# Order of the heads in the stored queries and keys, and loading of the staged tiles, in a transformer block

## The chip, the cores and the metric

The kernel runs on one core of one Trainium2 chip. The metric is the device time of one execution in microseconds. Five engines take part. TensorE (PE in the profile) multiplies matrices, VectorE (DVE) reduces and does elementwise work, ScalarE (ACT) copies and applies functions, GpSimd (POOL) takes some elementwise work, and SyncE (SP) issues most of the transfers between the main memory and the on-chip memory. Each engine works through its own instructions in order and waits on semaphores for the others.

## The reference

The program is one pre-norm transformer block in float32 on 2048 tokens of width 640, with 32 heads of 20 dimensions:

```
h   = x + softmax(q k^T / sqrt(20)) v @ wo        q, k, v = heads of layernorm(x) @ wqkv
out = h + (silu(z @ w_gate) * (z @ w_up)) @ w_down   with z = layernorm(h)
```

The softmax is over all 2048 keys, and every head needs the maximum of each row of scores.

## The kernel before

Precision is kept by splitting: a float32 matrix is written as a high and a low part, and a product is made of three partial products. A staged head holds three rows per dimension for the same reason, 60 rows in all, and two heads stand side by side on the partitions (rows 0 to 63 and 64 to 127), each with two positions along the free axis. So one tile holds one group of four heads.

The program has three stages: the projections (to about 362 us in the profile), the attention, and the feed-forward part. All that the change touches is in the projections and in the loads of queries and keys, `stack` (L111).

**Stage of projections.** The tokens are cut into four chunks `c` of 512. For each chunk the loop at L466 walks through 18 *slots*; slot number `18*c + j` is kept in `slot[0]` (L472). A slot is a "block" (`query_key`, L373: 15 matmuls of 512 columns that make 128 rows of queries or of keys) or a "value" (L414: 15 matmuls of 320 columns). Chunk 0 does blocks in slots 0 to 9 and values in slots 10 to 17; chunks 1 and 2 do likewise (18 to 27 and 28 to 35; 36 to 45 and 46 to 53); chunk 3 does its keys first (54 to 58), then values (59 to 66), then queries (67 to 71). After a block, `keep` (L395) copies the result to a tile `e`, splits it and hands it to `store` (L367), which issues it from ScalarE's queue at the next `keep`, to the DRAM tensor `qk_d`. There a group has 80 rows per part, sorted by dimension and, within it, by head.

**Row maxima beside the projections.** Part of the score maxima is computed during this stage, between the projections' matmuls. `max_pair` (L141) is one unit of it, called a pair below: two matmuls (L146) into one of three `ps_wide` buffers and a reduction on VectorE (L150). There are 208 pairs. `visit(n)` (L301) issues up to n of them from two queues: `urgent` (unit 0, from the tiles `k_stk` and `q_stk`) and `early`. A block has two visits of two pairs, after its tenth matmul and at its end; a value has one of three.

**Staged tiles.** For most `early` pairs, of head groups 1 to 7 and chunks 0 and 1, queries and keys are read back from `qk_d` into tiles `raw`. Their pool has four buffers, which also hold the raw weights early on (`load_w`, L311). A *set* (L238) is a group, a chunk of queries and a chunk of keys: 21 sets. `load_staged` (L254) takes two buffers per set and issues eight transfers, four by each of two calls of `stack`, all from SP's queue. The load of set i+1 is issued when the first pair of set i is issued (`first_keys`, L271), and not before the slot given by `ready_at` (L241). It uses the two buffers of set i-1, so SP waits for the last pair of that set. A set has 8 pairs, but only 4 or 6 where chunk 1 is set against the second chunk of keys. A pair whose slot has come is issued whether or not its tile has landed, and TensorE waits for it then. Queries of chunk 1 are loaded twice, once per set.

**The transfer.** In `stack`, a transfer of `n` partitions reads two heads per partition, `b` and `b + 2`: of the 4n stored rows of n dimensions it takes every second one, 2n rows at one even step, into n partitions of two pieces of 2 KB.

Of the kernel before, what the change touches and what calls it, by code (L numbers as in the profile page):

```python
# [29 lines left out]
G = 4  # L30
NG = H // G
# [12 lines left out]
def tile_block(ctx: ExitStack, tc: tile.TileContext, x, wqkv, wo, wg, wu, wd, out):  # L44
# [15 lines left out]
    def ps_wide():  # L60
        return psum.tile([P, 2, CH], F32, name="ps_wide", tag="ps_wide", bufs=3)
# [49 lines left out]
    def stack(dst, which, g, cs):  # L111

        src = qk_d[which, g].bitcast(F32).rearrange("i (d h) c -> (i d) h c", h=G)
        for b in range(2):
            heads = src[:, b::2, cs]
            both, first = ((DH, 0), (0, 2 * DH))[which]
            for row, n in ((both, 2 * DH), (first, DH)):
                nc.sync.dma_start(  # L118
                    dst[b * ROW + row : b * ROW + row + n].bitcast(F32), heads[:n]
                )  # L120
# [18 lines left out]
    mxs = {u: stk.tile([P, 2, 2, TPC, NC], F32, name=f"mx{u}") for u in range(NU)}  # L139

    def max_pair(mx, q, k, pair, t, kc, k0):  # L141

        ps = ps_wide()
        for b in range(2):
            rows = slice(b * ROW, b * ROW + NPART)
            nc.tensor.matmul(  # L146
                ps[:, b, :], q[rows, pair, t * P : (t + 1) * P], k[rows, pair, k0 : k0 + CH],
                start=True, stop=True,
            )
        nc.vector.tensor_reduce(mx[:, :, pair, t, kc], ps, axis=AX.X, op=ALU.max)  # L150
# [68 lines left out]
    with tc.tile_pool(name="pa", bufs=2) as pa:  # L219
# [14 lines left out]

        staged, slot, waiting_load = {}, [0], []
        sets = [(g, 0, 0) for g in range(1, NG)]  # L238
        sets += [(g, 1, kc) for g in range(1, NG) for kc in range(2)]

        def ready_at(g, c):  # L241

            block = ((g + 1) * GD - 1) // P
            return 2 * block + 6 if c == 0 else 18 * c + 9 + block

        def raw_tile():
            return pa.tile([P, ND, 2 * P], F32R, name="raw", bufs=4)

        def stage_tile():
            return raw_tile().rearrange("p a b -> p (a b)")[:, : 2 * CH].rearrange(  # L250
                "p (h n) -> p h n", h=2
            )

        def load_staged(i):  # L254
            g, c, kc = sets[i]
            k, q = stage_tile(), stage_tile()
            stack(k, 1, g, slice(kc * CH, (kc + 1) * CH))
            n = len(moved(g * NC + c, kc)) * P
            stack(q[:, :, :n], 0, g, slice(c * CH, c * CH + n))
            staged[i] = q, k  # L260

        def load_next(i):
            if i < len(sets):
                waiting_load.append(i)
                load_waiting()

        def load_waiting():
            if waiting_load and slot[0] + 1 >= ready_at(*sets[waiting_load[0]][:2]):
                load_staged(waiting_load.pop())

        def first_keys(i, t, pair):  # L271
            if t == 0 and pair == 0:
                load_next(i + 1)
            g, c, kc = sets[i]
            max_pair(mxs[g * NC + c], *staged[i], pair, t, kc, 0)

        def unit_keys(u, kc, t, pair):
            max_pair(mxs[u], queries[u], keys[0], pair, t, kc, kc * CH)
            if u == 0 and (kc, t, pair) == (NC - 1, TPC - 1, 1):
                max_all(0)  # L280

        def in_unit(u, kc, at):
            return [
                (at, lambda t=t, pair=pair: unit_keys(u, kc, t, pair))
                for t in moved(u, kc) for pair in range(2)
            ]

        def in_set(i):
            g, c, kc = sets[i]
            return [  # L290
                (ready_at(g, c), lambda t=t, pair=pair: first_keys(i, t, pair))
                for t in moved(g * NC + c, kc) for pair in range(2)
            ]

        urgent = [a for kc in range(NC) for a in in_unit(0, kc, 18 * kc + (6 if kc == 0 else 5))]
        early = [a for i in range(NG - 1) for a in in_set(i)]
        early += in_unit(1, 0, ready_at(0, 1)) + in_unit(1, 1, ready_at(0, 1))
        early += [a for i in range(NG - 1, len(sets)) for a in in_set(i)]
        early += in_unit(2, 0, ready_at(0, 2)) + in_unit(2, 1, ready_at(0, 2))

        def visit(n):  # L301
            load_waiting()
            for _ in range(n):
                for queue in (urgent, early):
                    if queue and queue[0][0] <= slot[0]:
                        queue.pop(0)[1]()
                        break

# [142 lines left out]
        for m, raw in enumerate(first_raw):  # L451
            cs = slice(m * P, (m + 1) * P)
# [5 lines left out]
        loaded = 5  # L458
# [7 lines left out]
        for c in range(NC):  # L466
            lns = []
            work = (some_keys + some_queries if c else first) + parts
            if c == NC - 1:
                work = some_keys + parts + some_queries  # L470
            for j, (kind, *which) in enumerate(work):
                slot[0] = 18 * c + j  # L472
                if c == 0 and j < 9:
                    for i in range(split_at[j], split_at[j + 1]):
                        split_w(i + 2)
                        if i % 2 == 1 and loaded < 8:
                            load_w(loaded)
                            loaded += 1
                if j == 0 and c + 1 < NC:
                    if c > 0:  # L480
                        load_x(c + 1)
                    lns = norm(c + 1)
                if which:
                    (query_key if kind == "block" else value)(c, *which)
                visit(2 if kind == "block" else 3)
                if c == 0 and j == ready_at(1, 0) - 1:
                    load_staged(0)
# [278 lines left out]
    u, o, r = tail.pop()  # L766
# [87 lines left out]
    ready = []  # L854
# [14 lines left out]
    g = gate(0, 0, gu[0][0])  # L869
# [5 lines left out]
    g = gate(0, 1, gu[0][0])  # L875
# [6 lines left out]
    g = gate(0, 2, gu[0][0], three[3])  # L882
# [97 lines left out]
```

## Time and profile before

| | us |
|---|---|
| median of three runs | 2201.95 (2201.9 to 2205.47) |
| the profiled execution | 2199.24 |
| its span | 2197.5 |
| TensorE busy / VectorE busy / ScalarE busy | 2140.9 / 1613.8 / 1278.1 |
| transfers read / written | 101.27 MB / 38.01 MB |

The span is cut into views: busy time by engine, busy tenths in 40 slices of some 55 us, the chain of work that ended last, groups of instructions with their mean durations, the waits by pair of instruction and releaser, and windows, which give each engine's busy time in a stretch. The granted clock is the share of full speed at which TensorE was allowed to run.

### The profile page before, as it was taken

How to read it: one execution, taken by the hardware profiler on the slowest of the kernel's cores; microseconds unless marked ns; L12 is line 12 of the kernel's file. 1: busy time of each engine (PE TensorE's matmuls, PEld its weight loads, DVE VectorE, ACT ScalarE, POOL GpSimd, SP SyncE). 2: the span in 40 equal slices, each digit the busy share in tenths (PEclk: the TensorE clock that was granted, in tenths of full speed). 3: DMA queues.
4: the chain of work that ended last, by engine and by line, in shares of the span. 5: the costliest groups of instructions: out<-in, count | busy, mean ns of one | idle time of the engine just before them, and what ended most of it. 6: DMA issues, size and time to landing. Idle time of an engine off the chain costs nothing.

```text
span 2197.5 us, 33889 instructions
## 1 busy us (share of the span) xinstructions
PE 2140.9 (97%) x12882; PEld 1258.5 (57%) x12882; DVE 1613.8 (73%) x2731; ACT 1278.1 (58%) x2486; POOL 317.0 (14%) x282
## 2 busy tenths in 40 slices
PE   7998998999999999999999999999999999999999
PEld 5765665333333333333333333345588888888888
DVE  6987985999999999999999999885353343453434
ACT  3222224899999999999999998886622111121110
POOL 5221212000000000000000000111213222122220
PEclk9998999999999999999999999999999999999999
DMA  7554543111210202102112112111221010010102
GB/s 237 181 162 140 175 138 93 51 41 31 61 43 26 78 24 66 45 24 67 37 32 72 31 59 64 35 57 51 75 62 43 19 30 24 19 31 19 30 19 96
DMA packets 125027, 142.29 MB, mean 65 GB/s; under 512 B 38880, under 2 KB 73584, under 8 KB 124864
## 3 DMA queue, kind: packets, MB, share of 16 engines
q1 hardware_dynamic: 110880, 113.36, 17.5%
q10 hardware_dynamic: 13984, 26.75, 4.0%
q8 instruction: 102, 1.67, 0.3%
q14 instruction: 61, 0.50, 0.1%
HBM read 101.27 MB, written 38.01 MB: 63 GB/s over the span
## 4 chain that ended last, share of the span: by engine, by line
PE 88%; DMA 4%; DVE 4%; SPq 1%; ACT 1%; issue 1%; POOL 0%; ACTq 0%; POOLq 0%; DVEq 0%
PE acc L646 23%; PE ps_a L830 17%; PE ps_max L156 15%; PE ps_one L636 13%; PE ps_b L916 9%; PE ps_one L381 3%; PE ps_one L422 2%; DVE mx L150 2%; PE ps_wide L146 2%; DMA raw<-qk_d 2%; PE ps_max L576 2%; PE ps_b L576 1%; SPq L118 1%; DMA qk_d<-e 1%; DVE mx L162 0%
## 5 line engine op out<-in xcount | busy, mean ns | idle before, releaser
L642 ACT ACTIVATE probs<-ps_one 128x512 f32<-128x512 f32 x2048 | 1044.7, 621 | 136.2 <-PE ps_one L636 135.4
L162 DVE TENSOR_REDUCE mx<-ps_max 128x1 f32<-128x512 f32 x1632 | 1020.4, 682 | 113.2 <-PE ps_max L156 77.9
L636 PE MATMUL ps_one<-q_stk,k_stk 62*128 62x512 f32 x2048 | 552.5, 423 | 6.6 <-ACT e L232 5.6
L646 PE MATMUL acc<-probs,v_stk 128*32 128x512 f32 x4096 | 548.0, 607 | 0.2
L156 PE MATMUL ps_max<-k_stk,q_stk 60*128 60x512 f32 x1632 | 543.4, 462 | 1.9 <-DVE mx L162 1.3
L156 PEld LDWEIGHTS ps_max<-k_stk,q_stk 60*128 60x128 f32 x1632 | 231.7, 185 | 431.7 <-DVE mx L162 412.6
L921 DVE TENSOR_TENSOR h<-ps_b,h 128x320 f32<-128x320 f32 x448 | 194.4, 485 | 311.9 <-PE ps_b L916 311.8
L636 PEld LDWEIGHTS ps_one<-q_stk,k_stk 62*128 62x128 f32 x2048 | 301.3, 186 | 85.0 <-ACT probs L642 51.9
L830 PE MATMUL ps_a<-z,gu_hi 128*128 128x512 f32 x1080 | 276.0, 393 | 0.6 <-ACT z L72 0.6
L150 DVE TENSOR_REDUCE mx<-ps_wide 128x2 f32<-128x1024 f32 x208 | 240.4, 1217 | 34.8 <-PE ps_wide L146 34.3
L830 PEld LDWEIGHTS ps_a<-z,gu_hi 128*128 128x128 f32 x1080 | 200.4, 188 | 42.2 <-ACT z L72 0.8
L72 ACT ACTIVATE y_hi<-s 128x512 fp32r<-128x512 f32 (+1 forms) x56 | 35.4, 632 | 254.0 <-DVE s L843 247.6
L646 PEld LDWEIGHTS acc<-probs,v_stk 128*32 128x32 f32 x4096 | 81.0, 108 | 160.7 <-issue 152.3
L838 ACT ACTIVATE s<-ps_a 128x512 f32<-128x512 f32 (+1 forms) x56 | 33.5, 598 | 198.5 <-PE ps_a L830 198.5
L830 PE MATMUL ps_a<-z,gu_lo 128*128 128x512 f32 x540 | 142.2, 393 | 0.0
L916 PE MATMUL ps_b<-d_hi,y_hi 128*128 128x320 f32 x448 | 139.0, 311 | 0.0
L916 PE MATMUL ps_b<-d_lo,y_hi 128*128 128x320 f32 x448 | 138.1, 309 | 0.0
L232 ACT ACTIVATE e<-ps_one 128x512 f32<-128x512 f32 x52 | 31.1, 598 | 180.0 <-DMA qk_d<-e 75.3
L916 PE MATMUL ps_b<-d_hi,y_lo 128*128 128x320 f32 x416 | 128.3, 308 | 0.0
L173 POOL CAST both<-neg 128x16 fp32r<-128x16 f32 x32 | 6.6, 207 | 834.5 <-DVE neg L169 393.4
L830 PEld LDWEIGHTS ps_a<-z,gu_lo 128*128 128x128 f32 x540 | 101.4, 188 | 23.1
L73 POOL TENSOR_TENSOR y_lo<-s,y_hi 128x512 fp32r<-128x512 f32 x52 | 68.0, 1309 | 269.4 <-ACT y_hi L72 269.4
(113 smaller groups left out, 1618.7 us busy)
## 6 DMA issues: line engine op xcount, KB each, us to landing
raw<-qk_d SPq DMA_DIRECT2D x70, 160.0 KB
k_stk<-qk_d SPq DMA_DIRECT2D x64, 160.0 KB
q_stk<-qk_d SPq DMA_DIRECT2D x64, 160.0 KB
qk_d<-e ACTq DMA_DIRECT2D x29, 320.0 KB
rb<-r_d SPq DMA_DIRECT2D x32, 256.0 KB
v_d<-ev ACTq DMA_DIRECT2D x16, 384.0 KB
raw<-qk_d SPq DMA_DIRECT2D x76, 80.0 KB
v_stk<-v_d SPq DMA_DIRECT2D x28, 192.0 KB
```

The lines of the kernel that those rows point to most:

```text
L73: lo_engine.tensor_tensor(out=lo, in0=src, in1=hi.bitcast(F32), op=ALU.subtract)
L150: nc.vector.tensor_reduce(mx[:, :, pair, t, kc], ps, axis=AX.X, op=ALU.max)
L156: nc.tensor.matmul(ps, queries[u][rows, pair, t * P : (t + 1) * P], keys[u // NC][rows, pair, kc * CH : (kc + 1) * CH], start=True, stop=True,
L162: nc.vector.tensor_reduce(mxs[u][:, b, pair, t, kc : kc + 1], ps, axis=AX.X, op=ALU.max)
L381: nc.tensor.matmul(ps, w[:, k, m * P : (m + 1) * P], a[:, k, :], start=(n == 0 and k == 0), stop=(n == 2 and k == ND - 1),)
L576: nc.tensor.matmul(ps[:, :HALF], a[:, k, :], w[:, k, hs], start=(n == 0), stop=(n == 3 * ND - 1),)
L636: nc.tensor.matmul(ps, keys[u // NC][rows, p, kt * P : (kt + 1) * P], queries[u][rows, p, :], start=True, stop=True,)
L642: nc.scalar.activation(probs[p][:, b, :], ps, AF.Exp, scale=scale)
L646: nc.tensor.matmul(acc[32 * j : 32 * j + 32, :], values[u // NC][:, kt, j * VW : j * VW + 32], probs[j // 2][:, j % 2, :], start=(kt == 0) ...
L830: nc.tensor.matmul(ps, a[:, i, k, :], b[:, k, :], start=(n == 0), stop=(n == 3 * ND - 1))
L916: nc.tensor.matmul(ps[:, :HALF], a[:, t * P : (t + 1) * P], b[:, hs], start=(n == 0), stop=(n == len(products) - 1),)
L921: nc.vector.tensor_tensor(out=h, in0=ps[:, :HALF], in1=h, op=ALU.add)
```

## The change

Three things change together.

1. The host sorts the columns of the query and key weights so that heads 0 and 2 of a group are stored next to each other, and 1 and 3 after them. `stack` then reads rows `2b` and `2b + 1` of each four. Which head stands where in a tile stays as it was.
2. Sets are replaced by *items*: one item is one tile, keys or queries of one group and chunk, loaded by four transfers. There are 35 items (two per group for chunk 0, three for chunk 1, whose queries are now loaded once, with all 512 columns). Item n is loaded when the pairs that use item n-4 have all been issued and its slot (`stored_at`) has come; this is looked up at every visit and after every staged pair.
3. A staged pair is issued only if both its tiles were loaded at least two slots earlier. If the pair at the head of a queue is not ready, the visit passes it by. The pairs of unit 0 come one slot later than before (`18*kc + 6`, and 7 in chunk 0).

```diff
-            heads = src[:, b::2, cs]
+            heads = src[:, 2 * b : 2 * b + 2, cs]
...
-            return 2 * block + 6 if c == 0 else 18 * c + 9 + block
+            if c == 0:
+                return 2 * block + 4
+            return 18 * c + 3 + block + (0 if which else ND)
...
-        def load_staged(i):
-            g, c, kc = sets[i]
-            k, q = stage_tile(), stage_tile()
-            stack(k, 1, g, slice(kc * CH, (kc + 1) * CH))
-            n = len(moved(g * NC + c, kc)) * P
-            stack(q[:, :, :n], 0, g, slice(c * CH, c * CH + n))
-            staged[i] = q, k
...
+        def load_items():
+            for n, (which, g, c, loaded, _) in enumerate(items):
+                if loaded is not None:
+                    continue
+                if slot[0] < stored_at(which, g, c) or (n >= 4 and users[n - 4]):
+                    return
+                t = raw_tile().rearrange("p a b -> p (a b)")[:, : 2 * CH].rearrange(
+                    "p (h n) -> p h n", h=2
+                )
+                stack(t, which, g, slice(c * CH, (c + 1) * CH))
+                items[n][3:] = t, slot[0]
+
+        def staged_keys(g, c, kc):
+            k, q = place[1, g, (c, kc)], place[0, g, c]
+
+            def one(t, pair):
+                max_pair(mxs[g * NC + c], items[q][3], items[k][3], pair, t, kc, 0)
+                for n in (k, q):
+                    users[n] -= 1
+                load_items()
+
+            def ready():
+                return all(items[n][3] is not None and slot[0] >= items[n][4] + 2 for n in (k, q))
...
-        urgent = [a for kc in range(NC) for a in in_unit(0, kc, 18 * kc + (6 if kc == 0 else 5))]
+        urgent = [a for kc in range(NC) for a in in_unit(0, kc, 18 * kc + (7 if kc == 0 else 6))]
...
+        early = [a for g in range(1, NG) for a in staged_keys(g, 0, 0)]
+        early += in_unit(1, 0, 28) + in_unit(1, 1, 28)
+        early += [a for g in range(1, NG) for kc in range(2) for a in staged_keys(g, 1, kc)]
+        early += in_unit(2, 0, 46) + in_unit(2, 1, 46)
...
         def visit(n):
-            load_waiting()
+            load_items()
             for _ in range(n):
                 for queue in (urgent, early):
-                    if queue and queue[0][0] <= slot[0]:
+                    if queue and queue[0][0]():
                         queue.pop(0)[1]()
                         break
...
-            qk = a[:, : 2 * D].reshape(D, 2, NG, G, DH).transpose(0, 1, 2, 4, 3)
+            qk = a[:, : 2 * D].reshape(D, 2, NG, 2, 2, DH).transpose(0, 1, 2, 5, 4, 3)
```

More of the change, by code (lines that the diff above doesn't have):

```diff
@@ L233, in split_sbuf, with stored_at @@
             split(copy, hi, lo, nc.gpsimd)
[L237 to L241, printed above, removed]
+        slot = [0]
+        items, place, users = [], {}, {}
+        def stored_at(which, g, c):
             block = ((g + 1) * GD - 1) // P
-            return 2 * block + 6 if c == 0 else 18 * c + 9 + block
+            if c == 0:
+                return 2 * block + 4
+            return 18 * c + 3 + block + (0 if which else ND)
@@ L246, in raw_tile @@
         def raw_tile():
             return pa.tile([P, ND, 2 * P], F32R, name="raw", bufs=4)
[L249 to L252, printed above, removed]
-        def load_staged(i):
-            g, c, kc = sets[i]
-            k, q = stage_tile(), stage_tile()
-            stack(k, 1, g, slice(kc * CH, (kc + 1) * CH))
-            n = len(moved(g * NC + c, kc)) * P
-            stack(q[:, :, :n], 0, g, slice(c * CH, c * CH + n))
-            staged[i] = q, k
@@ L262, in load_next, with stage @@
-        def load_next(i):
-            if i < len(sets):
-                waiting_load.append(i)
-                load_waiting()
[L267 to L275, printed above, removed]
+        def stage(use, which, g, c):
+            place[which, g, use] = len(items)
+            users[len(items)] = 0
+            items.append([which, g, c, None, None])
@@ new lines, in staged_keys @@
+        def staged_keys(g, c, kc):
[7 more added lines that the diff above has]
+                return all(items[n][3] is not None and slot[0] >= items[n][4] + 2 for n in (k, q))
+            pairs = [(t, pair) for t in moved(g * NC + c, kc) for pair in range(2)]
+            for n in (k, q):
+                users[n] += len(pairs)
+            return [(ready, lambda a=a: one(*a)) for a in pairs]
@@ L283, in in_unit @@
             return [
-                (at, lambda t=t, pair=pair: unit_keys(u, kc, t, pair))
+                (lambda: at <= slot[0], lambda t=t, pair=pair: unit_keys(u, kc, t, pair))
                 for t in moved(u, kc) for pair in range(2)
             ]
[L288 to L293, printed above, removed]
-        urgent = [a for kc in range(NC) for a in in_unit(0, kc, 18 * kc + (6 if kc == 0 else 5))]
[L296 to L299, printed above, removed]
+        for g in range(1, NG):
+            stage((0, 0), 1, g, 0)
+            stage(0, 0, g, 0)
+        for g in range(1, NG):
+            stage((1, 0), 1, g, 0)
+            stage(1, 0, g, 1)
+            stage((1, 1), 1, g, 1)
+        urgent = [a for kc in range(NC) for a in in_unit(0, kc, 18 * kc + (7 if kc == 0 else 6))]
[3 more added lines that the diff above has]
+        early += in_unit(2, 0, 46) + in_unit(2, 1, 46)
         def visit(n):
-            load_waiting()
+            load_items()
             for _ in range(n):
                 for queue in (urgent, early):
-                    if queue and queue[0][0] <= slot[0]:
+                    if queue and queue[0][0]():
                         queue.pop(0)[1]()
@@ L485, in tile_block @@
                 visit(2 if kind == "block" else 3)
-                if c == 0 and j == ready_at(1, 0) - 1:
-                    load_staged(0)
                 if c == 0 and j == 6:
```

## The prediction

> **What bounds the kernel now.** The page's busy rows come first. TensorE is at nine tenths or more almost everywhere, except in the first seven of 40 slices, which are the projections. A busy window inside the attention shows why nothing is looked for there.
>
> ```profile
> PE   7998998999999999999999999999999999999999
> DVE  6987985999999999999999999885353343453434
> 380.00:400.00 20.00, 20.00 (x139) 7.74 (x135) 18.63 (x31) 18.03 (x37) 0.42 (x2) 1.00 0.01 1
> ```
>
> Second, TensorE's waits up to 366 us (total, times, longest) tell what its gaps end on: the staged tiles' landing before all, VectorE next.
>
> ```profile
> PE ps_wide L146 <- DMA raw<-qk_d: 12.9, 10, 4.6
> PE ps_wide L146 <- DVE mx L150: 7.8, 5, 2.7
> PE ps_wide L146 <- issue: 1.8, 1, 1.8
> ```
>
> Third, the chain at the longest of them, in slot 34 (start, duration). SP got the free buffers at 173.91, issued a set's eight transfers one after the other, and the last landed 3.88 us after its issue had begun. Issuing took longer than landing.
>
> ```profile
> 173.44 0.92 PE ps_wide L146 x6
> ...
> 174.70 0.74 SPq L118
> ...
> 178.62 0.74 SPq L118
> ...
> 179.40 3.88 DMA raw<-qk_d
> ...
> 183.37 0.76 PE ps_wide L146
> ```
>
> Fourth, durations of an issue (min/median/max, ns): staged loads, then the stores to the same tensor.
>
> ```profile
> L118 SPq DMA_DIRECT2D raw<-qk_d x168: 738/742/1523, 40.1 to 301.9; - x168
> L370 ACTq DMA_DIRECT2D qk_d<-e x87: 309/454/932, 25.5 to 365.7; - x87
> ```
>
> Last, windows over the slots' starts (the first matmul of each group of 15, from the timeline): slots 6 to 12, 18 to 27, 28 to 35, 36 to 45, 46 to 53, 54 to 58. Columns: length, busy PE, PEld, DVE, ACT, POOL, granted clock, DMA share, GB/s.
>
> ```profile
> 38.93:77.65 38.72, 34.20 (x159) 22.91 (x160) 37.25 (x48) 10.91 (x18) 12.89 (x11) 0.96 0.65 194
> 95.66:152.63 56.97, 52.94 (x225) 33.68 (x223) 50.09 (x67) 11.06 (x18) 11.61 (x9) 0.97 0.55 167
> 152.63:189.54 36.91, 31.92 (x190) 25.90 (x188) 27.65 (x26) 10.79 (x20) 7.71 (x6) 0.91 0.49 159
> 189.54:253.22 63.68, 56.98 (x232) 35.38 (x230) 56.23 (x71) 11.07 (x18) 11.83 (x9) 0.92 0.53 159
> 253.22:286.21 32.99, 30.08 (x190) 23.93 (x188) 27.87 (x25) 10.90 (x20) 7.68 (x6) 1.00 0.55 174
> 286.21:313.36 27.15, 26.46 (x118) 16.47 (x116) 23.82 (x22) 5.11 (x9) 5.18 (x4) 1.00 0.53 159
> ```
>
> Two things are to be seen. Where the next chunk is normalised (slots 6 to 12, 18 to 25, 36 to 44) VectorE is nearly full. And the clock falls after a wait: it is 0.55 in slot 35, after 4.81 us, and 0.75 in slot 43, after 2.74 us. Undisturbed slots have fixed lengths: a block with four pairs 5.19 (slot 40), a block without pairs 3.43 (slot 68), a value with three pairs 3.69 at most (slot 33).
>
> **The change: the transfer.** Rows `2b, 2b+1` of four are no longer evenly spaced, so source and destination both read as n times two pieces, as in the stores of L370, instead of 2n against n times two. Stores with like sides issue in 309 to 454 ns mostly, but in the timeline those of 64 rows take 582 or more, so like sides alone don't decide. The 20-row `o_d` stores take 329. I take 0.45 us with its gap against 0.785 now; ends 0.35 and 0.785. The bytes per transfer stay, so I leave landing at 3.5 to 5.7 us from the last issue (the chain's pieces). By itself this is worth nothing on the path until a wait depends on it; it is priced there.
>
> In the Trainium skill, DMA: Bandwidth & Descriptors, section "Issuing engines are not separate DMA queues", the time to initiate a transfer is called usually small beside the transfer. By that rule the first edit would be worth zero; the trace differs here, with eight issues filling 6.2 us before a landing of 3.88.
>
> **Loads and waits.** 168 loads become 140 (35 tiles by four), 19.0 MB become 16.8. Following the planner's rules slot by slot, each load stands two slots or more ahead of its first pair: for the second keys of chunk 1 up to four slots. The closest is the queries of group 2, chunk 1: their buffer is freed by the second pair of slot 34 and they are wanted after the tenth matmul of slot 36, so 0.44 + 3.69 + 2.28 = 6.4 us remain. Four loads need 3 x 0.45 + 3.5 to 5.7 = 4.9 to 7.1, so a wait of up to 0.7; all such places together I take as 0.5 us (ends 0 and 5, the latter with slow issue and two cold slots of some 1.5 us). The waits of slots 12, 20, 34, 38, 46, 51 and 55 go. What is late next is VectorE.
>
> **What is queued behind.** SP now waits for the last user of a buffer, as it did; behind it stand the key and query loads of group 0, used three slots on, and the loads of x, used slots later. ScalarE's stores can wait for earlier loads in flight (ScalarE's copy L232 waited 18.7 us in four waits for staged loads); two projection buffers cover that, and TensorE waited 1.4 us in all for L232 in the blocks. If that cover went, 6.5 us, the longest, could fall on the path once.
>
> **Slots 6 to 12.** The four pairs of slot 6 leave. VectorE is the bound: its first reduction there starts at 46.90, behind the normalisation, and the 25th ends at 79.23, 37.25 busy of 38.72. With 21 pairs it ends 4 x 1.15 = 4.6 sooner. Ends: 0, and 6.7, by which slot 8 (55.33) can start sooner if slot 7 takes the place of 48.60. I take 4.6.
>
> **Slots 18 to 27.** VectorE works 5.17 in slots of 5.2. The 1.8 us wait of slot 20 left it idle as well, so 1.8 is gained; ends 0 and 3. Slot 24's wait of 2.2 us, for the normalisation's small operations, stays. The slot without pairs becomes 27 in place of 26: zero.
>
> **Slots 28 to 35.** Nothing else is full: 36.91 becomes 8 x 3.69 = 29.5, a gain of 7.4 (waits 4.81, the rest the clock). Ends 4.8 and 7.9.
>
> **Slots 36 to 45.** VectorE is idle for 63.68 - 56.23 = 7.45, of which 5.97 in slot 38; slot 42's wait of 2.74 remains. Gain 6.0; ends 4.0 (the wait of 3.96 alone) and 7.4.
>
> **Slots 46 to 53** become 8 x 3.69 = 29.5: 3.5 gained (ends 2.4 and 4.0). **Slots 54 to 58** become 5 x 5.19 = 26.0: 1.2.
>
> **Slot 67** gets the four pairs that slot 6 lost: 5.19 - 3.43 = 1.75 lost, since blocks alone stood there. No pair lies beyond it.
>
> **The attention** reads its tiles through the same `stack`; TensorE is busy 20.00 of 20 us there, so faster issue is worth nothing. If a load came late there, the cost would be as in slot 34, 7.6 us with the clock. The host's sort lies outside the time.
>
> Sum: 4.6 + 1.8 + 7.4 + 6.0 + 3.5 + 1.2 - 1.75 - 0.5 = 22.2 us. The profiled execution took 2199.24 (span 2197.5 and 1.7 around it), so 2177.0; it lies 2.7 under the median of 2201.95, and on the median the sum gives 2179.7.
>
> **The rivals.** *VectorE takes over.* If nothing is gained where VectorE is nearly full (slots 6 to 12, 18 to 27, 36 to 45), 7.4 + 3.5 + 1.2 - 1.75 - 0.5 = 9.9 remain: 2192. For it: 37.25 of 38.72. Against: in slot 38 VectorE stood idle for six microseconds.
>
> *The new shape issues no faster.* For it are the 64-row stores at 582 ns and more. Then 3 x 0.785 + 3.5 to 5.7 = 5.9 to 8.1 against 6.4 leaves the residual at its upper end, 5 in place of 0.5, and the sum at 17.7: 2184. The skill's rule on issue time cited above, by which a shorter issue changes little, would end at the same 17.7.
>
> *Hidden anyway.* SP's own waits show 45.6 us for stores to `qk_d` to land, in 18 waits. If loads start when stores land, moving them earlier does nothing: 2200. Against: at slots 34, 38 and 51 SP waited for the buffer and then issued without a pause.
>
> *Slower.* The new loads stand in SP's queue before buffers are free, and ScalarE's stores wait for loads in flight; if the copies behind them hold TensorE, each tile costs time. From 22.2 / 35 = 0.63 us per tile on, the change is slower than before; at 1 us per tile it ends at 2214.9. For it: the 18.7 us of L232. Against: those four waits, up to 6.5 us, left TensorE 1.4 us of waiting, and there are fewer loads.
>
> **How the numbers follow.** About 0.2%, 4.4 us, is what a measurement of this kernel can tell from no change. Forecast 0.56 (2174 to 2187 on its own), VectorE 0.14, no faster issue 0.12, a gain above the sum's ends 0.04: all faster, 0.86. Hidden anyway 0.07, slower 0.07. The likeliest gives 2179.7. The range goes from 2172 (upper ends in slots 6 to 12, 28 to 35 and 36 to 45 together: 2.1 + 0.5 + 1.4, and some clock) to 2194, just over the VectorE rival; 0.82 lies inside.
>
> **What would show it.** Issues at L118 near 0.45 us, 140 on `raw`; TensorE's wait for `raw` from 12.9 to under 2 us; the granted clock in the windows of slots 28 to 35 and 46 to 53 at 1.00 and both near 29.5 us long; waits for L150 still 6 to 12 us; the attention starting some 22 us sooner than 364.8. Wrong would be: `raw` still first among the waits, waits for L150 doubled, or L232 grown past 5 us.

## The result, and the profile after

The changed kernel takes 2180.48 us (median of four runs, 2175.53 to 2184.03); the kernel before, run beside it, 2201.93 (2198.18 to 2205.47). The ratio is 0.9901, with a 95% interval of 0.9875 to 0.9927: about 21 us faster. The profiled execution of the changed kernel took 2179.47 (span 2177.5), 19.8 less than the profiled one of before. Lines behind the edit have moved: the block's matmul L381 is L389 now, the value's L422 is L430, the store L370 is L378, and L636 is L642.

First the busy rows of the page. Of the seven thin slices at the start, the fourth and the seventh have gained a tenth on TensorE and the third has lost one; a slice of 54 us is too coarse to show more.

```profile
PE   7989999999999999999999999999999999999999
DVE  7988996999999999999999998884353433443434
```

TensorE's waits up to 390 us (total, times, longest) answer to those of before. The staged tiles have fallen from 12.9 us in ten waits to 3.1 in two. In their place stands the value's matmul waiting for ScalarE's copy L232, 4.6 us; the last line, 1.1 us, is a pair in slot 39 too. L642 is the first matmul of the attention. Before, the lines for L232 were these (and 0.2 us at the value's L422):

```profile
PE ps_one L636 <- ACT e L232: 5.6, 1, 5.6
...
PE ps_one L381 <- ACT e L232: 1.4, 2, 1.2
```

After:

```profile
PE ps_wide L146 <- DVE mx L150: 6.0, 5, 1.9
PE ps_one L430 <- ACT e L232: 4.6, 2, 3.9
PE ps_one L642 <- ACT e L232: 4.5, 1, 4.5
PE ps_wide L146 <- DMA raw<-qk_d: 3.1, 2, 2.7
PE ps_one L389 <- ACT e L232: 1.3, 1, 1.3
PE ps_wide L146 <- DMA qk_d<-e: 1.1, 1, 1.1
```

The issues of the staged loads (min/median/max, ns) went from 742 to 334 in the median, 140 instead of 168.

```profile
L118 SPq DMA_DIRECT2D raw<-qk_d x140: 273/334/1512, 38.4 to 282.8; - x140
```

Last the windows of the same slots as before: 6 to 12, 18 to 27, 28 to 35, 36 to 45, 46 to 53, 54 to 58 (length, busy PE, PEld, DVE, ACT, POOL, granted clock, DMA share, GB/s).

```profile
37.94:71.06 33.12, 30.32 (x151) 21.14 (x152) 32.57 (x43) 10.93 (x18) 12.82 (x11) 1.00 0.68 205
89.17:142.92 53.75, 51.41 (x224) 32.44 (x222) 52.08 (x69) 10.45 (x18) 10.38 (x8) 1.00 0.59 179
142.92:177.03 34.11, 30.13 (x189) 25.04 (x189) 24.89 (x22) 11.51 (x21) 8.99 (x7) 0.95 0.41 134
177.03:239.36 62.33, 56.63 (x233) 35.12 (x231) 54.74 (x70) 11.32 (x19) 11.59 (x9) 0.92 0.58 175
239.36:268.31 28.95, 28.87 (x191) 23.72 (x189) 27.77 (x26) 10.65 (x20) 7.71 (x6) 1.00 0.51 162
268.31:294.31 26.00, 26.00 (x118) 16.28 (x116) 23.72 (x22) 4.92 (x8) 5.18 (x4) 1.00 0.53 154
```

Two of the windows have a clock of 1.00 and a TensorE that is idle for 0.08 us at most (46 to 53, 54 to 58). Two are not: 28 to 35 at 0.95, and 36 to 45 at 0.92 and hardly shorter than before. By stage, the 19.8 us are made up so:

| slots | before, us | after, us | gain | predicted |
|---|---|---|---|---|
| up to slot 0 | 16.83 | 15.80 | 1.0 | 0 |
| 6 to 12 | 38.72 | 33.12 | 5.6 | 4.6 |
| 18 to 27 | 56.97 | 53.75 | 3.2 | 1.8 |
| 28 to 35 | 36.91 | 34.11 | 2.8 | 7.4 |
| 36 to 45 | 63.68 | 62.33 | 1.35 | 6.0 |
| 46 to 53 | 32.99 | 28.95 | 4.0 | 3.5 |
| 54 to 58 | 27.15 | 26.00 | 1.15 | 1.2 |
| 67 | 3.55 | 5.18 | -1.6 | -1.75 |

Of the slots left out, 0 to 5, 13 to 17 and 59 to 66 changed by less than 0.2 us each; 68 to 71 together gained 1.5. The attention starts 19.0 us sooner, at 345.8 instead of 364.8, and all that follows takes 1831.6 instead of 1832.6.

**The new wait in slots 28 and 29.** The chain around it (start, duration): a store of `e` is 5.90 us from its issue to its landing, and ScalarE's next copy L232 into that buffer waits for it; the fifteen matmuls of a value wait for the copy, which frees their PSUM tile.

```profile
142.28 0.61 ACT e L232
...
143.55 5.90 DMA qk_d<-e
...
149.55 0.61 ACT e L232
...
150.20 3.97 PE ps_one L430 x15
```

There are two buffers `e`, and a block's store is issued only at the next block's `keep`; so a buffer filled every second block has less than one block, 5.2 us, for its store. Between 105 and 150 us seven of the eight copies into `e` that the trace holds were released by a landed store, with up to 7.5 us from one to the next. Before, six of ten were, between 100 and 156 us, but TensorE hardly waited for them.

**The new wait in slot 39.** ScalarE's queue issues a store at the start of slot 38 (chain, first fence). SP's timeline, with TensorE's behind it (second fence; in brackets the idle time before an instruction and what ended it): SP issues nothing from 188.2 to 192.4, though the buffer for the next staged tile is free at 187.5, when the last pair that reads it ends; then its seven loads take 7.59 us, with a stop until 193.6 and another until 199.3 among them. TensorE, which wants that tile in slot 39, waits 2.73 and then 1.06.

```profile
187.61 0.33 ACTq L378
...
187.98 5.59 DMA qk_d<-e
```

```profile
186.90 1.30 SPq L228 DMA_DIRECT2D xt<-in_A_x  x3
192.36 7.59 SPq L118 DMA_DIRECT2D raw<-qk_d  x7
...
197.70 0.58 PE L146 MATMUL ps_wide<-raw 60*128 60x512 f32 x1 [2.73 <-DMA raw<-qk_d]
199.34 1.19 PE L146 MATMUL ps_wide<-raw 60*128 60x512 f32 x3 [1.06 <-DMA qk_d<-e]
```

In the trace's semaphore records, the transfers of SP's and of ScalarE's queue share eight completion semaphores, and each of the 140 staged loads carries a wait for its own semaphore, that is, for the landing of the transfer that used it last. The load that stopped until 193.6 was due on the semaphore of the store issued at 187.98, which landed at 193.57; the load before it, on that of the store issued at 187.61, which landed at 192.30. Both stores hold chunk 2 and the loads read chunk 1, so a load can be late because of stores that have nothing to do with it. What SP waits in all for stores to `qk_d` ahead of L118 rose from 45.6 us to 72.4; but the planner alone (below) had 42.2 with the same wait in slot 39, so this sum doesn't measure it.

### The profile page after: what moved, and what is told of

The parts are those of the page before. It is cut to its first block, busy times and chain, and to the rows that moved or that the text cites. A ratio compares the mean times of both kernels' runs of the same rounds, so it can differ in the third digit from the quotient of the medians.

```text
span 2177.5 us, 33846 instructions
## 1 busy us (share of the span) xinstructions
PE 2133.4 (98%) x12882; PEld 1254.7 (58%) x12882; DVE 1612.2 (74%) x2731; ACT 1278.2 (59%) x2486; POOL 316.6 (15%) x282
## 4 chain that ended last, share of the span: by engine, by line
PE 89%; DVE 7%; DMA 3%; ACT 1%; issue 0%; SPq 0%; ACTq 0%; POOL 0%; DVEq 0%; POOLq 0%
PE acc L652 23%; PE ps_a L836 17%; PE ps_max L156 15%; PE ps_one L642 14%; PE ps_b L922 9%; DVE mx L150 4%; PE ps_one L389 3%; PE ps_one L430 2%; PE ps_wide L146 2%; PE ps_max L582 2%; DMA qk_d<-e 1%; PE ps_b L582 1%; DVE mx L162 0%; PE ps_one L357 0%; DMA wo_raw<-in_A_wo 0%
## 5 line engine op out<-in xcount | busy, mean ns | idle before, releaser
L642 PE MATMUL ps_one<-q_stk,k_stk 62*128 62x512 f32 x2048 | 553.0, 424 | 5.0 <-ACT e L232 4.5
L642 PEld LDWEIGHTS ps_one<-q_stk,k_stk 62*128 62x128 f32 x2048 | 301.2, 186 | 83.9 <-ACT probs L648 51.5
L150 DVE TENSOR_REDUCE mx<-ps_wide 128x2 f32<-128x1024 f32 x208 | 239.6, 1215 | 22.7 <-PE ps_wide L146 22.6
L836 PEld LDWEIGHTS ps_a<-z,gu_hi 128*128 128x128 f32 x1080 | 200.4, 188 | 42.2 <-ACT z L72 0.8
L232 ACT ACTIVATE e<-ps_one 128x512 f32<-128x512 f32 x52 | 31.1, 598 | 168.4 <-DMA qk_d<-e 75.1
```

The costliest lines, as they stand in the source:

```text
L642: nc.tensor.matmul(ps, keys[u // NC][rows, p, kt * P : (kt + 1) * P], queries[u][rows, p, :], start=True, stop=True,)
L836: nc.tensor.matmul(ps, a[:, i, k, :], b[:, k, :], start=(n == 0), stop=(n == 3 * ND - 1))
```

## The experiments

The theory after the comparison: the gain comes from loads that are issued two slots ahead; what is missing from it is held by ScalarE's stores, in slots 28 and 29 through the buffer `e`, in slot 39 through the shared semaphores. The rivals: faster issue is what gained; or the late stores are an old cost that has nothing to do with the change.

### One part of the change alone

*The layout alone*: before, with heads side by side.

```diff
-            heads = src[:, b::2, cs]
+            heads = src[:, 2 * b : 2 * b + 2, cs]
...
-            qk = a[:, : 2 * D].reshape(D, 2, NG, G, DH).transpose(0, 1, 2, 4, 3)
+            qk = a[:, : 2 * D].reshape(D, 2, NG, 2, 2, DH).transpose(0, 1, 2, 5, 4, 3)
```

> The old planner with sets, but the heads of a row half side by side. Theory (the staged loads are late because eight issues take 6.2 us): an issue at L118 falls from 0.74 to about 0.34 us, a set is complete 7 x 0.4 = 2.9 us sooner, the wait of slot 34 falls from 4.81 to about 1.9 and that of slot 38 from 3.96 to about 1.1, the small ones vanish; TensorE's wait for raw 12.9 -> 3 us, 8 to 13 us gained, 2189 to 2194. Rival (issue is hidden beside the transfer, which takes its 4 to 6 us anyway): waits for raw stay above 10 us, 2198 to 2204.

Measured: 2193.61 us, ratio 0.9946 (0.9928 to 0.9963), some 12 us gained. From its trace, TensorE's wait and the issues:

```profile
PE ps_wide L146 <- DMA raw<-qk_d: 10.0, 6, 3.9
```

```profile
L118 SPq DMA_DIRECT2D raw<-qk_d x168: 273/336/1403, 40.1 to 294.8; - x168
```

So the layout by itself is what makes the issue short, with 168 transfers as before. It takes 742 ns to 336, and it gains by itself. The time lies where it was expected, but the waits don't: 10.0 of 12.9 us for staged tiles stay instead of 3, among them 3.0 us in slot 34 and 3.9 in slot 38. In its profiled execution the attention starts 7.8 us sooner, and slots 36 to 45 are no shorter (64.48 us). By which waits the layout gains its 12 us stays open.

*The planner alone*: the changed kernel with the old layout (the diff above the other way round).

> The new planner, items and two-slot gate, with every second stored row read as before (issue 0.74 us). Theory (two slots of lead cover even slow issues, except where the buffer comes free late): waits for raw 3 to 6 us in place of 3.1 with the new layout, 14 to 19 us gained against before, 2183 to 2188. Rival (the short issue carries the gain, the planner only moves work): at most 8 us gained, 2194 or more.

Measured: 2179.95 us, ratio 0.9892 (0.987 to 0.9914); the changed kernel stood at 0.9901 and, run again as a control in another comparison, at 2180.55 and 0.9903 (0.9881 to 0.9926).

```profile
PE ps_wide L146 <- DMA raw<-qk_d: 4.6, 2, 3.0
PE ps_one L430 <- ACT e L232: 3.0, 1, 3.0
```

```profile
L118 SPq DMA_DIRECT2D raw<-qk_d x140: 738/742/1763, 40.8 to 286.8; - x140
```

With issues of 742 ns the planner gives the whole gain, more than was expected of it (14 to 19 us), and the same two residual waits, in slots 39 and 29. The two parts don't add: by the ratios 12 and 24 us alone, 22 together, and the last two agree within their intervals. The planner takes most of the waits for staged tiles away with slow issues too (4.6 of 12.9 us stay); the layout alone leaves most of them. What of the planner does it, the earlier issue, the fewer loads or the passing by of pairs that aren't ready, no run separates.

The control was sent with this:

> The changed kernel once more, beside the others on one chip. 2175 to 2184 as before; slots 6 to 12 between 33 and 38 us if that stage varies between executions of one program, and near 33.1 if it does not; a wait for L232 of 3 to 5 us in slots 28 or 29 and a wait of 2 to 5 us in slot 39.

Slot 39 waited as expected (4.6 us); the wait for L232 in slots 28 and 29 came to 0.32 us only, not 3 to 5. The control tells something else too: its slots 6 to 12 took 38.59 us, not 33.12, its slots 18 to 27 56.65 and its slots 28 to 35 28.89:

```profile
154.25:183.14 28.89, 28.52 (x189) 23.42 (x188) 24.90 (x22) 10.89 (x20) 7.72 (x6) 1.00 0.38 124
```

Stages of one and the same program vary by several microseconds from one execution to the next, while the medians agree within 0.1 us. So what one profile shows of a stage is no proof of what an edit did there.

### Where the missing gain went

*A third buffer for the stores*: every third block uses the third tile in all chunks, as in chunk 0 (in the last chunk only those of even `m`).

```diff
-            if c == 0 and m % 3 == 2:
+            if m % 3 == 2 and (c < NC - 1 or m % 2 == 0):
```

> The changed kernel, with the third buffer for projected blocks (it lies in v_stk and was used in chunk 0 only) used for every third block of all chunks, except for the queries of chunk 3. Theory (what took the place of the waits for raw is the store chain: two buffers e, each free only when its store has landed, 5 to 6 us after the next block's copy): TensorE's wait for L232 in slots 28 and 29 (4.6 us) and the slow clock after it vanish, slots 28 to 35 fall from 34.1 to about 29.5, 4 to 8 us faster than the changed kernel, 2172 to 2177. Rival (ScalarE is held by transfers that share a completion semaphore with staged loads, not by the buffer): the waits for L232 stay or move, 2178 to 2183.

Measured: 2176.37 us, ratio 0.9877 (0.9852 to 0.9903). The wait of slots 28 and 29 is gone, and slots 28 to 35 are at the floor:

```profile
151.43:180.31 28.88, 28.73 (x190) 23.45 (x188) 24.80 (x22) 10.89 (x20) 7.70 (x6) 1.00 0.38 125
```

Slot 39 kept its waits (3.77 and 0.51), so this buffer isn't what holds it. For slots 28 and 29 this profile is not enough, since the control was at 28.89 without the buffer. The profiles together say more: of the four with two buffers and late stores from ScalarE (the changed kernel, the control, the planner alone, and unit 0's pairs at their old slots, below) three waited 2.2 to 4.6 us for L232 there and one 0.32; of the five under the new planner with a third buffer or with stores issued at once none waited. The gain over the changed kernel, 4 us, is no more than the intervals allow.

*The third buffer in the kernel before.*

> The kernel before, with the third buffer for projected blocks in all chunks. Theory (the store chain became the limit only when the waits for raw had gone): nothing to gain, 2199 to 2206, waits for raw stay at 10 to 15 us, slots 28 to 35 at 36 to 37.5 us. Rival (the store chain also set when the staged loads of the old planner could start): waits for raw fall by half or more, 2190 to 2196.

Measured: 2204.58 us, ratio 1.0005 (0.9987 to 1.0022): nothing. In its profiled execution the waits for `raw` were even longer (18.2 us in nine waits). So the wait for `e` is one that the change uncovered; that the waits for `raw` had left the stores time is the likely reason, not a measured one.

*Unit 0's pairs at their old slots.*

```diff
-        urgent = [... in_unit(0, kc, 18 * kc + (7 if kc == 0 else 6))]
+        urgent = [... in_unit(0, kc, 18 * kc + (6 if kc == 0 else 5))]
```

> The changed kernel with the pairs of unit 0 back at their old slots (6 in chunk 0, 18*kc + 5 later). Theory (VectorE bounds slots 6 to 12): slots 6 to 12 take 4 to 5 us more, slot 67 1.6 us less, 2 to 4 us slower than the changed kernel in all, 2182 to 2185. Rival (the gain of slots 6 to 12 comes from the earlier loads, not from the four pairs that left): slots 6 to 12 within 1 us of the changed kernel's 33.1, 2178 to 2180.

Measured: 2186.48 us, ratio 0.9922 (0.9898 to 0.9946). The median is 6 us above that of the changed kernel, but the intervals overlap, and its slots 6 to 12, where the four pairs came back, took 37.97 us, which lies inside what the changed kernel itself shows (33.1 and 38.6). So the 4.6 us of slot 6 are neither confirmed nor refuted. Slot 67 stayed at 5.19 us, against the expectation: by the planner's rules the four pairs leave slot 26, not slot 67, and slots 18 to 27 have 217 matmuls in the trace instead of 224.

*Stores issued at once, still from ScalarE's queue.*

```diff
-            while stores:
-                queue.dma_start(*stores.pop(0))
-            stores.extend(last)
+            for piece in last:
+                queue.dma_start(*piece)
```

> The changed kernel with each store issued from ScalarE's queue in its own block, not in the next. ScalarE then waits for GpSimd's split (1.3 us) before the issue. Theory (two buffers e are enough if the store starts 3 us or more sooner): waits for L232 in slots 28 and 29 gone, slots 28 to 35 at 29 to 30; the wait of slot 39 stays (the semaphores are shared as before) or shrinks, 2172 to 2178. Rival (ScalarE's wait for GpSimd and for the loads' semaphores holds up its copies): L232 waits grow above 6 us, 2182 to 2195.

Measured: 2186.07 us, ratio 0.9924 (0.9902 to 0.9945): the median is some 6 us worse than the control's, though the intervals overlap. Slots 28 to 35 are at 28.87, as with the third buffer. But ScalarE now waits for the split at each store, and its copies come late in slots 4 to 7 (waits of 1.28 to 2.41 us; slots 0 to 5 took 27.75 us against 22.15). Slot 39 still waited, 2.27 and 1.86 us.

*Stores issued at once, from GpSimd's queue*, which makes the split itself. The values' stores move with them.

```diff
-        def store(*last, queue=nc.scalar):
-            while stores:
-                queue.dma_start(*stores.pop(0))
-            stores.extend(last)
+        def store(*last, queue=nc.gpsimd):
+            for piece in last:
+                queue.dma_start(*piece)
```

> The changed kernel with the stores to qk_d and v_d issued from GpSimd's queue, each right behind its own split, in place of ScalarE's queue one block later. They then share no completion semaphore with SP's loads. Theory (loads and stores hold each other up through the eight semaphores that both queues use in turn, and the buffer e comes free late): the waits for L232 in slots 28 and 29 and for raw in slot 39 (4.6 and 3.8 us) both vanish, slots 28 to 35 at 29 and 36 to 45 at 55 to 57 us, 2166 to 2173. Rival (landing times are set by the transfers themselves, and GpSimd is slow to issue): slot 39 keeps its wait, or GpSimd's issues delay its splits, 2178 to 2195.

Measured: 2168.95 us, ratio 0.985 (0.9827 to 0.9872), better than both kernels. Among TensorE's waits `raw` is gone. The windows are slots 28 to 35 and 36 to 45.

```profile
PE ps_wide L146 <- DVE mx L150: 5.8, 5, 1.8
PE ps_one L388 <- ACT v_stk L232: 2.8, 1, 2.8
PE ps_one L641 <- ACT e L232: 1.3, 1, 1.3
```

```profile
146.52:175.41 28.89, 28.75 (x189) 23.44 (x187) 25.16 (x23) 10.90 (x20) 11.54 (x14) 1.00 0.33 116
175.41:230.01 54.60, 52.70 (x232) 32.86 (x231) 53.47 (x70) 11.58 (x19) 24.48 (x32) 1.00 0.71 206
```

Two things differ from both profiles of the changed kernel. Slots 36 to 45 are 7.7 us shorter than in the one and 8.6 than in the other. And the last wait of the stage, the attention's first matmul for L232, fell from 4.5 and 4.6 us to 1.3; slots 68 to 71 took 15.30 us instead of 18.51 and 18.59. Together that is 11 to 12 us, about what the median gained (11.5). Slots 28 to 35 are as long as in the control.

*Stores from GpSimd's queue, but one block late*, as the changed kernel has them. It separates the two causes: the stores from GpSimd's queue use eight other semaphores in the trace, so those of SP's loads are no longer shared with them, but the buffer `e` is freed late.

```diff
-        def store(*last, queue=nc.scalar):
+        def store(*last, queue=nc.gpsimd):
```

> The changed kernel with the stores issued from GpSimd's queue, but one block late as from ScalarE. Loads and stores share no semaphores, while the buffer e comes free as late as before. If the shared semaphores were what held the loads of slot 39: no wait for raw there, slots 36 to 45 at 55 to 57 us. If the late start of the stores was what held ScalarE's copies at slots 27 to 29: a wait for L232 of 1 to 5 us stays there or at slot 71; 2169 to 2176 in all. If the start of the stores is all that counts: slot 39 keeps 3 to 5 us, 2177 to 2183.

Measured: 2221.87 us, ratio 1.0076 (1.0061 to 1.0091), slower than before and far above both times that were expected, as is the length of slots 36 to 45, 67.99 us. No wait for `raw` is left, slot 39 takes 5.21 us with none; its tile's load went out at 206.02, as soon as the buffer was free at 206.00, and slots 37 and 38 had not been stretched (5.20 and 5.19 us). But every store stands behind the split of the following block in GpSimd's order, and ScalarE's copies wait for them everywhere (TensorE's waits, then ScalarE's):

```profile
PE ps_one L389 <- ACT e L232: 19.2, 9, 3.8
PE ps_one L430 <- ACT e L232: 15.8, 5, 5.5
PE ps_one L642 <- ACT e L232: 10.4, 1, 10.4
```

```profile
ACT e L232 <- DMA qk_d<-e: 157.4, 26, 10.0
```

Both halves of the theory are borne out, each in its place, though not in their price: with the stores on another queue slot 39's load is on time even though they start late, and with late stores the copies wait. That the sharing held the load is read from the semaphores in the trace; no run changed the sharing alone, so that something else about GpSimd's queue helped isn't excluded.

*Stores from GpSimd's queue at once, with the old layout*, and *in the kernel before*:

> Stores from GpSimd at once, new planner, but every second stored row read as before (issue 0.74 us). If two slots of lead hide the issues: within 3 us of the same kernel with short issues (2169), 2166 to 2173. If the short issue matters once nothing else holds the loads: waits for raw of 2 us or more come back at slots 36 or 39, with the clock 4 to 10 us, 2173 to 2180.

> The kernel before with stores from GpSimd at once. If the old planner's loads are late because a set is issued only when its buffers come free: waits for raw of 9 us or more stay, slots 28 to 35 at 35 us or more, and only the end of the stage (slots 67 to 71) and some of slot 6 shorten, 2188 to 2198. If it was the shared semaphores that made them late: waits for raw under 4 us, 2172 to 2182.

Measured: 2167.97 us with the planner and the old layout, ratio 0.983 (0.9814 to 0.9846), so faster issue adds nothing where loads are two slots ahead. In the kernel before, 2189.8 us, ratio 0.993 (0.9916 to 0.9945): 16 us gained, but the waits for staged tiles stay, and slots 28 to 35 remain at 36.70.

```profile
PE ps_wide L146 <- DMA raw<-qk_d: 11.7, 9, 4.0
```

Most of the old plan's late loads are thus its own, and not the stores'.

*VectorE's normalisation in parts.* With the stores from GpSimd at once, the longest waits left in slots 24 and 42 are for VectorE's small operations. They are handed out over three slots instead of one.

```diff
-                + [lambda: rs.append(rstd_of(pa, mv[:, :, 1], TPC, "a"))]
+                + refine
...
+        return r, [lambda: (begin(), refine()), refine, refine]
```

> Stores from GpSimd at once, changed planner and layout, and the 14 small operations of the normalisation's reciprocal root handed out in three parts over three slots instead of in one. If the waits for L150 in slots 24 and 42 (1.8 us each, with the slow clock after them) come from that burst on VectorE: they vanish, 3 to 7 us less than 2169, 2162 to 2166. If VectorE's total work is the bound: nothing, 2166 to 2171.

Measured: 2168.16 us, ratio 0.9828 (0.9814 to 0.9843), the same as without it within the intervals. The waits of slots 24 and 42 fell from 1.81 each to 0.27 and 0.24, slots 18 to 27 and 36 to 45 became 3.1 us shorter together, but the profiled execution lost about as much in other stages (slots 46 to 53 30.07 against 29.01, a start 1.0 later), and the attention starts at 333.1 instead of 333.3. Whether the 3 us would be kept on average, these runs don't show.

## Why the prediction was right, and where not

Forecast 2179.7, measured 2180.48: the sign and the size came out, and the mechanism in the main, since the waits for staged tiles went and the experiment with the planner alone shows that this carries the gain. What the prediction named as its signs mostly came: 140 issues on `raw`, at 334 ns rather than 450; waits for L150 at 6.0 us, within 6 to 12; the attention 19.0 us sooner against some 22; `raw` no longer first. Others failed: the wait for `raw` ended at 3.1 and not under 2, and slots 28 to 35 took 34.1 us at a clock of 0.95, not 29.5 at 1.00. The waits for L232 within the projections grew from 1.6 us (1.4 at blocks, 0.2 at a value) to 5.9 (1.3 and 4.6), past the 5 that was to mean a wrong account. It was wrong in this part, as the next paragraphs show. And the sum was right partly by luck: in the profiled execution its own terms gave 16.5 of 22.2 us, and 3.5 more came from places for which it had no term, 1.0 at the start, 1.5 in slots 68 to 71 and 1.0 after the stage.

**Slots 46 to 53, 54 to 58, 67** were right within 0.5 us: 4.0, 1.15 and -1.6 against 3.5, 1.2 and -1.75. Here nothing but late loads had stood in the way, and the floors of undisturbed slots (3.69 and 5.19 us) applied; slots 46 to 53 went a little below theirs.

**Slots 28 to 35** was one of two large misses, 2.8 for 7.4. The floor was right: it was reached in the control (28.89), with a third buffer and with GpSimd's stores. The step that failed is "two projection buffers cover that". With the pairs on time the stores' chain through two buffers `e` came late next, and TensorE waited 0.68 and 3.92 us for L232 in slots 28 and 29. The prediction had looked for stores held by loads in flight; here the copies waited for their own buffers' stores. Its price if the cover went, 6.5 us once on the path, was of the same order. Since the control waited only 0.32 there, this loss comes and goes between executions.

**Slots 36 to 45**: 1.35 for 6.0, and 0.5 in the control (63.17). The step that failed is the residual of 0.5 us for all loads that come close: slot 39 alone waited 2.73 + 1.06, and with the slow clock behind it took 11.84 us instead of 5.2. "Ends 0 and 5" had allowed for that; the value taken did not. The closest place was sought by when a buffer is freed and how long four issues take, and found in slot 36, which didn't wait. The load that was late had a free buffer and stood behind two stores' completion semaphores. SP's 45.6 us of waiting for stores to land were weighed only as a reason for no gain at all, not as a wait that could grow.

**Slots 6 to 12 and 18 to 27** gave 5.6 and 3.2 for 4.6 and 1.8, in this execution. In the control they gave 0.1 and 0.3. So these two agreements are partly chance, and the same goes for the microsecond at the start. In the two profiles of the changed kernel the length of slots 6 to 12 goes with VectorE's busy time (last section); that VectorE bounds them is argued, since with stores issued at once from ScalarE they took 37.88 us with VectorE busy for 32.00.

**The transfer.** The issue came to 334 ns, near the lower end given. That it is worth nothing on the path with the new planner is shown twice: the planner with issues of 742 ns stood at 0.9892 against 0.9901, and with GpSimd's stores at 0.983 against 0.985. By the Trainium skill, "DMA: Bandwidth & Descriptors", section "Issuing engines are not separate DMA queues", which calls the time to initiate a transfer usually small, it should be so; the runs agree with that outcome once loads have two slots of lead, and not before (the layout alone gained 12 us).

**The rivals.** *No faster issue* fell by its premise, yet its arithmetic, 17.7 us with a residual of 5, would not have been borne out either: the planner with the slow issue lost nothing. *Hidden anyway* fell: the loads were early and TensorE's waits went. *VectorE takes over* holds for some executions and not for the median: in the control's profiled execution slots 6 to 12, 18 to 27 and 36 to 45 gained next to nothing, VectorE's waits were 9.3 us, and the attention started 11.7 us sooner (353.1), where the rival said 9.9; with 2185.83 us it was the longest of its four. But what held its slots 36 to 45 was the load of slot 39, 2.65 and 1.95 us, more than VectorE. *Slower* fell, though its mechanism, loads and stores holding each other and the copy L232 behind them, is the one that took back the gain. In this profile it cost 4.6 us of waiting for L232 and, with the clock, some 6.6 in slot 39, 11 us in all or 0.3 per tile: half of the 0.63 from which it decides. (At 1 us per tile the prediction's sum gives 2214.7, not 2214.9.) With GpSimd's late stores, which lengthen the same wait, the kernel did end slower than before.

## What to carry to other kernels

When a wait is taken away, look at what was using the time it gave: a chain with two buffers whose transfer takes as long as the work between them comes due next, and a wait of one queue for another queue's transfers, invisible in the buffers, moves with the plan. In this kernel, issuing a store when its data is ready, from the engine that makes the data, instead of one step late from an engine that others wait for, was worth another 11.5 us; the other queue without the earlier issue cost some 40 instead. A stage's gain in one profiled execution is to be held against a second profile of the same kernel before it is explained.

## What was not expected of the hardware

**The issue time of a staged load goes with its shape.** A transfer of staged rows whose two sides have the same form issued in 334 to 344 ns (median), one that reads 2n evenly spaced rows into n times two pieces in 742, with the same bytes. Like sides are not all: ScalarE's stores of 64 rows, with like sides too, took 596 ns or more in the changed kernel. From GpSimd's queue the same stores took 510 to 804 ns:

```profile
L378 POOL DMA_DIRECT2D qk_d<-e x89: 510/602/804, 25.7 to 337.6; - x89
```

**Small VectorE operations beside GpSimd.** In slots 6 to 12 the normalisation's operations on 128x4 values take 0.16 us each, and some of them up to 2.5 in the changed kernel and 3.5 with GpSimd's stores. In the control's timeline (start, duration; VectorE's first, GpSimd's behind the dots) the long ones lie where GpSimd works on tiles in SBUF:

```profile
47.61 0.16 DVE L86 TENSOR_TENSOR t_a<-t_a,v_a 128x4 f32<-128x4 f32 x1
47.81 2.52 DVE L87 TENSOR_SCALAR t_a<-t_a 128x4 f32<-128x4 f32 x1
50.36 1.46 DVE L88 TENSOR_TENSOR r_a<-r_a,t_a 128x4 f32<-128x4 f32 x1
...
47.65 1.29 POOL L73 TENSOR_TENSOR e<-e 128x512 fp32r<-128x512 f32 x1 [1.69 <-ACT e L72]
48.87 1.43 POOL L496 MEMSET ev<- 128x768 f32 x2
50.25 1.55 POOL L73 TENSOR_TENSOR w_lo<-raw,w_hi 128x640 fp32r<-128x640 f32 x1
```

L87 ends at 50.33, as GpSimd's zeroing does (50.30); L88 ends at 51.82, as its subtraction does (51.80). With the same 43 instructions VectorE was busy 32.57 us in slots 6 to 12 in the one profile of the changed kernel and 36.51 in the other: which operations meet GpSimd's differs between executions, and these 3.9 us go with a stage that was 5.5 longer. The Trainium skill, "SBUF — State Buffer", section "SBUF: two separate sides", says that VectorE and GpSimd share a pair of ports, held by one for a whole instruction while the other is blocked, and that VectorE needs them for an operation in a two-port mode or, against a GpSimd operation that reads SBUF, for one with two inputs in SBUF. The trace agrees for L88, which has two inputs and is held by some 1.3 us beside a subtraction; L87 has one input and is held by some 2.3 us beside zeroing, and whether it runs in such a mode the trace doesn't say. The same page warns, in that section, that transfers issued by GpSimd starve while a VectorE operation in such a mode holds these ports; here, with VectorE busy 53.47 of 54.60 us in slots 36 to 45, no issue from GpSimd took over 0.81 us, and over the whole kernel the stores landed 2.2 to 7.6 us after their issue. Most of VectorE's work there reduces `ps_wide`, so this may not be the case that the page means.

**The clock falls after short waits.** Stretches of 7 us from about the end of a wait show it. Before, behind 2.74 us in slot 42:

```profile
236.00:243.00 7.00, 7.00 (x26) 4.39 (x25) 6.80 (x7) 1.69 (x3) 1.27 (x1) 0.76 0.43 130
```

After, behind 1.28 us in slot 24 and 1.91 in slot 42:

```profile
127.73:134.73 7.00, 7.00 (x31) 4.60 (x32) 7.00 (x7) 1.23 (x2) 1.53 (x2) 1.00 0.45 136
221.88:228.88 7.00, 7.00 (x25) 4.45 (x25) 6.14 (x7) 1.23 (x2) 1.27 (x1) 0.76 0.59 184
```

A wait of 1.9 us cost a quarter of the clock for the 7 us behind it, 7 x 0.24 = 1.7 us, nearly as much again; one of 1.3 cost nothing, and neither did one of 1.81 in slot 24 with GpSimd's stores, where the clock was 1.00. The length alone doesn't decide: behind 1.74 us in slot 24 with the third buffer the clock was 0.76 over 7 us, behind 1.85 with GpSimd's stores and the old layout 1.00. The Trainium skill, "TensorE: Matmul & The Clock Gate", section "HAM oscillation — how this bites in real kernels", gives gaps over about 3.4 us as what is to be avoided; these rows show the clock falling after less.
